# A decode layer on one core: shared weights kept on TensorE, w1 loaded early, the last value products placed by landing, the last cast on two engines

## The chip, the cores and the metric

The kernel runs on one core of a Trainium2 chip. The metric is the device time of one execution in microseconds (us); the kernel before takes 529.73 us (median of three runs, 529.25 to 531.3). The profile's own span, from the first to the last instruction, is some 2.1 us shorter than the time (527.6 us in the profiled run of before); I keep the two apart and call them "time" and "span".

## The reference

A parallel block in one decode step: attention over the last 2048 of 8192 cached positions, a SwiGLU feed-forward net, and the residual, for four sequences of one token each.

```python
B, D, H, Sk, Dh, F = 4, 640, 32, 8192, 192, 1536     # bf16 throughout
xn = layernorm(x)                                     # [4, 640]
W  = min(4096, max(256, Sk // 4))                     # 2048
q  = xn @ wq                                          # [4, 32*192]
k, v = k_cache[:, :, Sk-W:], v_cache[:, :, Sk-W:]     # [4, 32, 2048, 192] each
o  = softmax(q . k * Dh**-0.5) . v                    # per head
out = x + o @ wo + (silu(xn @ w1) * (xn @ w3)) @ w2   # [4, 640]
```

K and V are 4 x 32 x 2048 x 192 x 2 bytes = 100.7 MB each. With the weights the kernel reads 222.97 MB and does little arithmetic with them.

## The kernel before

K and V of one head are 3.1 MB each and come in one transfer per head, K into two buffers, V into three. For each head the scores are made in four quarters: VectorE multiplies K with the broadcast q, TensorE adds the six slices of 32 products by matmuls with the identity, VectorE reduces the remaining 32.

```python
def mult(u):                       # u = head*4 + quarter; VectorE, 1.75 us
    pr = ppool.tile([P, JQ, Dh], BF16, tag="pr")
    nc.vector.tensor_tensor(out=pr[:], in0=kts[h][:, g*JQ:(g+1)*JQ, :], in1=qbc[...], op=ALU.mult)

def adder(u):                      # TensorE: six matmuls, all with the same weights idb
    for kk in range(NK):
        nc.tensor.matmul(ps[:], lhsT=idb[:], rhs=pr[:, :, kk*DD:(kk+1)*DD],
                         start=(kk == 0), stop=(kk == NK-1))

def pv(h, j0=0, j1=NJ):            # 32 value products, weights = the head's probabilities z
    for jj in range(j0//2, j1//2):
        nc.tensor.matmul(o_ps[c*CT:c*CT+2*B, :], lhsT=z[:, 2*jj:2*jj+2, :], rhs=vt[:, 2*jj:2*jj+2, :], ...)
    ...
    nc.scalar.copy(out=o_sb[:], in_=o_ps[:])
```

All instructions are placed by hand in slots, one slot per quarter (128 of them and a tail). Within a slot a phase number orders them. Each engine gets its instructions in this order. The parts of the schedule that the change touches:

```python
ends = {H-3: (NU-1, NU+1), H-2: (NU+2, NU+3), H-1: (NU+6, NU+7)}   # slots of pv, ge_sum
for h in range(H):
    if h >= KBUFS: add((h-KBUFS+1)*GQ, 0, load_k, h)
    if h < H-2:    add(u0+2, 0, load_v, h)
    ...
    v, m = ends.get(h, (u0+L, u0+L+1))
    # h < H-1: add(v, 7, pv, h);  the last head in two halves, slots v-1 and v
    add(m, 7, ge_sum, h)
f = FFN_HEAD * GQ                          # FFN_HEAD = 6
add(f, 0, ffn_load, "w1", B_w1);     add(f+7, 7, ffn_in, "w1")
add(f+8, 0, ffn_load, "w3", B_w3);   add(f+15, 7, ffn_in, "w3")
... # at the end, in this order on the queue: V30, V31 (two halves), w2 part 0, wo 6, wo 7, w2 parts 1 and 2
res = ppool.tile([NR, N0], BF16, tag="pr", name="res")
nc.vector.tensor_copy(out=res[:], in_=acc[0:NR, :])
nc.sync.dma_start(out=out_v[:, 0:N0], in_=res[0:B, :])
nc.scalar.dma_start(out=out_v[:, N0:D], in_=res[CT:NR, :])
```

The last two heads are 30 and 31; "K31", "pv30" and so on name their loads and products. In the profile's names `kt` is K, `vt` is V, `pr` the products, `ps` the adder's sums, `o_ps` the value products, `acc` the final sum; both feed-forward input weights and w2 appear as `w`.

Of the kernel before, what the change touches and what calls it, by code (L numbers as in the profile page):

```python
# [12 lines left out]
ALU = mybir.AluOpType  # L13
ACTF = mybir.ActivationFunctionType
AX = mybir.AxisListType


@with_exitstack
def kernel(
# [15 lines left out]
    VBUFS: int = 3,  # L35
    PBUFS: int = 4,
    L: int = 8,
    FFN_HEAD: int = 6,
):
    nc = tc.nc  # L40
    P = 128
    B, Sq, D = A_x.shape
    _, H, Sk, Dh = A_k_cache.shape
# [4 lines left out]
    PB = P // B  # L48
    NJ = W // PB
    GQ = 4  # L50
# [8 lines left out]
    NU = H * GQ  # L59
    N0 = D // 2  # L60
# [4 lines left out]
    assert (H * Dh) % QC == 0 and NQ % 6 == 0 and QW % P == 0 and Dh == CT * RPP and P == HG * CT and F == HG * CT * FC  # L65
    assert 2 * H * Dh <= NJ * Dh and KBUFS == 2 and VBUFS == 3

    ctx.enter_context(tc.manual_schedule())
    head = ctx.enter_context(tc.tile_pool(name="head", bufs=1))
    fpool = ctx.enter_context(tc.tile_pool(name="ffn", bufs=1))  # L70
# [15 lines left out]
    v_win = A_v_cache[:, :, Sk - W:Sk, :]  # L86
    kts, vts, prs, pss, scs, exs, zs = {}, {}, {}, {}, {}, {}, {}
# [5 lines left out]
                          in_=k_win[:, h].rearrange("b (p j) d -> p b (j d)", p=PB))  # L93
        kts[h] = kt

    def load_v(h, parts=1):
        vt = vpool.tile([P, NJ, Dh], BF16, tag="vt")
        src = v_win[:, h].rearrange("b (p j) d -> p b j d", p=PB)
        n = NJ // parts
        for j in range(0, NJ, n):  # L100
            nc.sync.dma_start(out=vt[:, j:j + n, :].rearrange("q j d -> q (j d)"),
                              in_=src[:, :, j:j + n, :].rearrange("p b j d -> p b (j d)"))
        vts[h] = vt

    def wo_load(hg):
# [8 lines left out]
    for k0 in range(0, KC, 2):  # L114
        n = min(2, KC - k0)
        wt = vpool.tile([P, 2, H * Dh], BF16, tag="vt")
        nc.sync.dma_start(out=wt[:, 0:n, :].rearrange("p k n -> p (k n)"),
                          in_=wq_v[:, k0:k0 + n, :].rearrange("p k n -> p (k n)"))
        wq_rows += [wt[:, i, :] for i in range(n)]
    for h in range(KBUFS):  # L120
# [9 lines left out]
    mask_f = const.tile([P, B], FP32, name="mask_f")  # L130
    nc.vector.tensor_reduce(out=mask_f[:], in_=idf[:].rearrange("q (p b) -> q b p", b=B), axis=AX.X, op=ALU.add)
    mask_b = const.tile([P, B], BF16, name="mask_b")
# [3 lines left out]
    nc.vector.tensor_reduce(out=rows[:], in_=idf[:].rearrange("q (c k) -> q k c", k=CT)[:, 0:2 * B, :],  # L136
                            axis=AX.X, op=ALU.add)
    NREP = CT // B
# [8 lines left out]
    ssum = const.tile([B, 1], FP32, name="ssum")  # L147
    nc.vector.tensor_reduce(out=ssum[:], in_=xf[:], axis=AX.X, op=ALU.add)
    negmean = const.tile([B, 1], FP32, name="negmean")
# [40 lines left out]
    o_banks = []  # L190
    for i in range(2):
        o_ps = ps_o.tile([P, 2 * Dh], FP32, tag="o_ps", name="o_ps")
# [3 lines left out]
    acc = ps_acc.tile([P, N0], FP32, name="acc")  # L196
# [37 lines left out]
    def reduce_quarter(u):  # L234
        h, g = u // GQ, u % GQ
        if g == 0:
            scs[h] = small.tile([P, NJ], FP32, tag="sc", name="sc")
        nc.vector.tensor_reduce(out=scs[h][:, g * JQ:(g + 1) * JQ], in_=pss.pop(u)[:], axis=AX.X, op=ALU.add)  # L238

    def chain_lmax(h):  # L240
        lmax = small.tile([P, 1], FP32, tag="lmax")
        nc.vector.tensor_reduce(out=lmax[:], in_=scs[h][:], axis=AX.X, op=ALU.max)  # L242
        chs[h] = [lmax]
# [6 lines left out]
    def chain_gmax(h):  # L250
        gmax = small.tile([1, B], FP32, tag="gmax")
        nc.vector.tensor_reduce(out=gmax[:], in_=chs[h][1][0:1, 0:P].rearrange("o (p b) -> o b p", b=B),  # L252
                                axis=AX.X, op=ALU.max)
        gneg = small.tile([1, PB, B], FP32, tag="gneg")
# [20 lines left out]
                                in1=mask_b[:].unsqueeze(1).to_broadcast([P, NJ, B]), op=ALU.mult)  # L275
        zs[h] = z

    def pv(h, j0=0, j1=NJ):
        o_ps, z, vt = o_banks[h % 2], zs[h], vts[h]
        for jj in range(j0 // 2, j1 // 2):  # L280
            c = jj % 4
            nc.tensor.matmul(o_ps[c * CT:c * CT + 2 * B, :], lhsT=z[:, 2 * jj:2 * jj + 2, :],  # L282
                             rhs=vt[:, 2 * jj:2 * jj + 2, :], start=(jj < 4), stop=(jj >= NJ // 2 - 4))
        if j1 < NJ:
            return
        zs.pop(h)
        vts.pop(h)
        o_sb = small.tile([P, 2 * Dh], FP32, tag="o_sb", bufs=2, name="o_sb")
        nc.scalar.copy(out=o_sb[:], in_=o_ps[:])  # L289
        o_sbs[h] = o_sb  # L290
# [76 lines left out]
    def add(slot, phase, fn, *args):  # L367
        sched[slot].append((phase, len(sched[slot]), fn, args))



    ends = {H - 3: (NU - 1, NU + 1), H - 2: (NU + 2, NU + 3), H - 1: (NU + 6, NU + 7)}
    for h in range(H):
        u0, ul = h * GQ, h * GQ + GQ - 1
        if h >= KBUFS:
            add((h - KBUFS + 1) * GQ, 0, load_k, h)
        if h < H - 2:
            add(u0 + 2, 0, load_v, h)
        for u in range(u0, ul + 1):
            add(u, 1, mult, u)  # L380
            add(u + 1, 2, adder, u)
            add(u + 1, 8, reduce_quarter, u)
        add(ul + 1, 9, chain_lmax, h)
        add(ul + 2, 3, chain_tr, h)
        add(ul + 2, 4, chain_gmax, h)
        add(ul + 3, 3, chain_bc, h)
        add(ul + 3, 4, chain_z, h)
        add(ul + 4, 5, ge_tot, h)
        if h % HG == HG - 1:
            add(ul + 4, 9, ge_rec, h // HG)  # L390
        v, m = ends.get(h, (u0 + L, u0 + L + 1))
        if h < H - 1:
            add(v, 7, pv, h)
        else:
            add(v - 1, 7, pv, h, 0, NJ // 2)
            add(v, 7, pv, h, NJ // 2, NJ)
        add(m, 7, ge_sum, h)
        if h % HG == HG - 1:
            add(m + 1, 0, ge_turn, h // HG)
    e = ends[H - 1][1] + 1  # L400
    for hg in range(NG - 2):
# [1 line left out]
        add(hg * HG * GQ + 8, 0, wo_load, hg)  # L403
        add(a, 6, ge_proj, hg, 0, RPP // 2)
        add(a + 1, 6, ge_proj, hg, RPP // 2, RPP)
    f = FFN_HEAD * GQ
    add(f, 0, ffn_load, "w1", B_w1)
    add(f + 7, 7, ffn_in, "w1")
    add(f + 7, 9, ffn_silu)
    add(f + 8, 0, ffn_load, "w3", B_w3)  # L410
    add(f + 15, 7, ffn_in, "w3")
    add(f + 15, 9, ffn_h)
    add(8, 0, x_load)
    add(16, 6, x_add, 0)
    add(17, 6, x_add, 1)


    for h in range(H - 2, H):
        add(NU - 6, 0, load_v, h, 1 + (h == H - 1))
    add(NU - 6, 0, w2_load, 0)  # L420
    add(NU - 6, 0, wo_load, NG - 2)
    add(NU - 6, 0, wo_load, NG - 1)
# [11 lines left out]

    NR = CT + B
    res = ppool.tile([NR, N0], BF16, tag="pr", name="res")
    nc.vector.tensor_copy(out=res[:], in_=acc[0:NR, :])
    out_v = out.rearrange("b s d -> (b s) d")
    nc.sync.dma_start(out=out_v[:, 0:N0], in_=res[0:B, :])
    nc.scalar.dma_start(out=out_v[:, N0:D], in_=res[CT:NR, :])  # L440
# [30 lines left out]
```

## Time and profile before

| | before |
|---|---|
| time, median of 3 | 529.73 us |
| span | 527.6 us |
| TensorE / VectorE busy | 67% / 65% |
| data queue, share of 16 DMA engines | 98.6% |
| bytes read | 222.97 MB |

The profile page of before, cut: busy time and instructions of TensorE (PE), bandwidth in 40 equal slices of the span, the DMA queues (packets, MB, share of 16 engines), and the adder's weight loads (busy us, mean ns | idle before, and what ended it).

```profile
span 527.6 us, 5428 instructions
PE 353.5 (67%) x2306; PEld 142.6 (27%) x2307; DVE 345.6 (65%) x435; ACT 45.6 (9%) x143; POOL 1.1 (0%) x8
...
GB/s 358 434 430 415 420 439 434 430 434 419 439 438 427 432 427 437 429 434 428 432 432 432 432 427 435 432 432 430 432 430 432 432 430 434 429 435 427 438 419 203
...
q1 hardware_dynamic: 11680, 222.97, 98.6%
q8 instruction: 18, 0.29, 0.2%
...
L230 PEld LDWEIGHTS <-idb 128*128 128x128 bf16 x768 | 74.4, 102 | 258.7 <-issue 200.1
```

The stream of data is the kernel: all slices but the first and the last show 415 to 439 GB/s, and 222.97 MB at 431 GB/s take about 517 of 527.6 us. The instruction queue q8, with its 18 packets (16 KiB and 0.88 to 0.97 us each in the trace), looks like nothing.

Windows of before around 40 us (columns: window, its length, busy us of each engine, granted clock, DMA share, GB/s):

```profile
40.00:44.00 4.00, 2.24 (x10) 0.87 (x9) 3.97 (x5) 0.00 (x0) 0.00 (x0) 1.00 0.91 369
44.00:48.00 4.00, 2.72 (x13) 1.25 (x12) 3.97 (x6) 0.27 (x2) 0.00 (x0) 1.00 1.06 455
```

From 40 to 44 us the rate falls to 369 GB/s: there is a hole. The same view at the end:

```profile
518.00:519.00 1.00, 1.00 (x20) 0.40 (x16) 0.17 (x1) 0.00 (x0) 0.00 (x0) 1.00 0.99 405
519.00:520.00 1.00, 0.99 (x17) 0.35 (x8) 0.00 (x0) 0.00 (x0) 0.00 (x0) 1.00 0.68 284
...
521.00:522.00 1.00, 1.00 (x24) 0.71 (x18) 0.00 (x0) 0.00 (x0) 0.00 (x0) 1.00 0.49 195
522.00:523.00 1.00, 0.65 (x11) 0.20 (x6) 0.80 (x2) 0.00 (x0) 0.00 (x0) 1.00 0.13 45
523.00:524.00 1.00, 0.95 (x15) 0.62 (x16) 0.00 (x0) 0.00 (x0) 0.00 (x0) 1.00 0.03 13
```

Here the 16 engines do not stop together. The share goes from 0.99 to about 0.5 near 519 us (seven of them are done), stays there for over two microseconds, and a last engine works alone until 523.5 us. What TensorE and VectorE do meanwhile, from the timeline of before (start us, us, engine, line, operation, operands, count, and in brackets the idle time before and what ended it):

```profile
490.16 1.47 PE L230 MATMUL ps<-pr,idb 128*128 128x512 bf16 x6
...
498.64 1.76 DVE L219 TENSOR_TENSOR pr<-kt,qbc 128x3072 bf16<-128x3072 bf16 x1 [2.71 <-DMA kt<-in_A_k_cache_dram]
...
513.82 2.73 PE L282 MATMUL o_ps<-vt,z 128*8 128x384 bf16 x32
...
524.62 0.48 DVE L437 CAST res<-acc 36x320 bf16<-36x320 f32 x1 [1.62 <-PE acc L200]
525.13 0.30 SPq L439 DMA_DIRECT2D out_dram<-res  x1
```

The first line is one adder: six matmuls in 1.47 us. K31 lands at 498.64 us. The 32 products of pv30 take 2.73 us from 513.82 on (the granted clock is 0.50 from 514 to 516 us), pv31, the sums and the projection come behind them, and the last cast starts at 524.62, over 1.1 us after the last byte. The chain of waits of before (start, us, what) says the same: it ends in computation, not in a transfer.

```profile
522.62 0.39 DVE oT L315
...
523.05 1.54 PE acc L200 x20
...
524.62 0.48 DVE res L437
```

### The profile page before, as it was taken

Reading aid. Unit: us, or ns where it says so; the run is one execution under the profiler, and the core shown is the slowest. Engines: PE = TensorE matmul, PEld = TensorE weight load, DVE = VectorE, ACT = ScalarE, POOL = GpSimd, SP = SyncE. Lnnn points to the kernel's source line nnn. Section 1 sums busy time; section 2 is a strip of 40 time slices with the busy share of each in tenths; the row PEclk is TensorE's granted clock in tenths of the full one; section 3 lists DMA queues with packets and bytes.
Section 4 is the critical chain, followed back from the end, with each engine's and each line's share of the span. In section 5 each row is a group of like instructions: output and inputs, shape, how many; then the busy total and the mean of one; then the engine's idle time right before and its main releaser. Section 6 shows DMA issues by size and latency. Waiting matters only on the chain.

```text
span 527.6 us, 5428 instructions
## 1 busy us (share of the span) xinstructions
PE 353.5 (67%) x2306; PEld 142.6 (27%) x2307; DVE 345.6 (65%) x435; ACT 45.6 (9%) x143; POOL 1.1 (0%) x8
## 2 busy tenths in 40 slices
PE   2865886765657476577637866577566777675686
PEld 0322332322212232223212322223222332232233
DVE  3179775776458567686637876577657867677661
ACT  2111000100211000000000000000000000000010
POOL 0000000000000000000000000000000000000000
PEclk9889887899878989789997998789997988799788
DMA  8999999999999999999999999999999999999994
GB/s 358 434 430 415 420 439 434 430 434 419 439 438 427 432 427 437 429 434 428 432 432 432 432 427 435 432 432 430 432 430 432 432 430 434 429 435 427 438 419 203
DMA packets 11719, 223.31 MB, mean 423 GB/s; under 512 B 1312, under 2 KB 1328, under 8 KB 2608
## 3 DMA queue, kind: packets, MB, share of 16 engines
q1 hardware_dynamic: 11680, 222.97, 98.6%
q8 instruction: 18, 0.29, 0.2%
q14 instruction: 5, 0.04, 0.0%
q10 hardware_dynamic: 16, 0.01, 0.0%
HBM read 222.96 MB, written 0.01 MB: 423 GB/s over the span
## 4 chain that ended last, share of the span: by engine, by line
DMA 57%; DVE 22%; PE 18%; ACT 2%; issue 1%; SPq 0%
DMA kt<-in_A_k_cache_dram 54%; DVE pr L219 15%; PE ps L230 9%; PE po L307 4%; DVE sc L238 3%; DMA wt<-in_A_wq_dram 3%; PE qps L179 2%; PE o_ps L282 2%; DVE z L274 1%; ACT ex L266 1%; PE mt L260 1%; DVE oT L315 1%; DVE og L312 0%; PE acc L200 0%; ACT L266 0%
## 5 line engine op out<-in xcount | busy, mean ns | idle before, releaser
L230 PE MATMUL ps<-pr,idb 128*128 128x512 bf16 x768 | 208.5, 412 | 152.3 <-DVE pr L219 152.3
L219 DVE TENSOR_TENSOR pr<-kt,qbc 128x3072 bf16<-128x3072 bf16 x128 | 223.5, 1746 | 113.9 <-DMA kt<-in_A_k_cache_dram 113.9
L230 PEld LDWEIGHTS <-idb 128*128 128x128 bf16 x768 | 74.4, 102 | 258.7 <-issue 200.1
L238 DVE TENSOR_REDUCE sc<-ps 128x16 f32<-128x512 f32 x128 | 87.2, 681 | 2.0 <-PE ps L230 2.0
L282 PE MATMUL o_ps<-vt,z 128*8 128x384 bf16 x1024 | 60.6, 373 | 2.7 <-DMA vt<-in_A_v_cache_dram 2.7
L307 PE MATMUL po<-o_sb,sel_w 128*32 128x192 f32 x128 | 49.1, 517 | 1.1 <-ACT o_sb L289 1.1
L282 PEld LDWEIGHTS <-z 128*8 128x8 bf16 x1024 | 26.2, 94 | 32.8 <-issue 22.8
L289 ACT COPY o_sb<-o_ps 128x384 f32<-128x384 f32 x32 | 15.3, 479 | 189.7 <-PE o_ps L282 189.7
L274 DVE TENSOR_TENSOR z<-ex,mask_b 128x256 bf16<-128x256 bf16 x32 | 13.5, 422 | 22.0 <-ACT ex L266 22.0
L263 ACT COPY negm<-mt 128x1 f32<-128x1 f32 x32 | 5.1, 159 | 259.0 <-PE mt L260 259.0
L307 PEld LDWEIGHTS po<-o_sb,sel_w 128*32 128x32 f32 x128 | 13.6, 128 | 26.8 <-issue 25.0
L179 PE MATMUL qps<-wt,xnT 128*128 128x512 bf16 x59 | 17.2, 456 | 4.8 <-DMA wt<-in_A_wq_dram 4.7
L185 DVE CAST qbc<-qps 128x512 bf16<-128x512 f32 x6 | 3.8, 684 | 18.7 <-PE qps L179 18.7
L260 PEld LDWEIGHTS mt<-ones_ff,gneg 1*128 1x128 f32 x64 | 9.5, 186 | 13.8 <-issue 11.7
L252 DVE TENSOR_REDUCE gmax<-mt 1x4 f32<-1x128 f32 x32 | 8.8, 275 | 6.6 <-PE mt L247 6.6
L260 PE MATMUL mt<-ones_ff,gneg 1*128 1x1 f32 x64 | 12.2, 258 | 0.0
L247 PE MATMUL mt<-idf,lmax 128*1 128x128 f32 x32 | 10.6, 330 | 1.1 <-DVE lmax L242 1.1
L266 ACT ACTIVATE ex<-sc,negm 128x64 bf16<-128x64 f32 x32 | 11.1, 348 | 1.0
L179 PEld LDWEIGHTS <-xnT 128*128 128x128 bf16 x60 | 6.7, 112 | 14.8 <-issue 9.7
L200 PE MATMUL acc<-wo_t,oT 128*4 128x320 bf16 x96 | 9.2, 298 | 0.4 <-DVE oT L315 0.4
L294 PEld LDWEIGHTS po<-rsum,tot_w 128*32 128x32 f32 x64 | 4.6, 110 | 14.1 <-issue 12.5
L242 DVE TENSOR_REDUCE lmax<-sc 128x1 f32<-128x64 f32 x32 | 7.0, 220 | 1.1
(52 smaller groups left out, 64.2 us busy)
## 6 DMA issues: line engine op xcount, KB each, us to landing
kt<-in_A_k_cache_dram SPq DMA_DIRECT2D x32, 3072.0 KB, 19.0
vt<-in_A_v_cache_dram SPq DMA_DIRECT2D x31, 3072.0 KB, 26.1
wo_t<-in_A_wo_dram SPq DMA_DIRECT2D x8, 960.0 KB, 20.5
wt<-in_A_wq_dram SPq DMA_DIRECT2D x2, 3072.0 KB, 13.3
w<-in_B_w_dram SPq DMA_DIRECT2D x2, 1920.0 KB, 27.1
vt<-in_A_v_cache_dram SPq DMA_DIRECT2D x2, 1536.0 KB, 31.2
wt<-in_A_wq_dram SPq DMA_DIRECT2D x1, 1536.0 KB
w<-in_B_w_dram SPq DMA_DIRECT2D x1, 1280.0 KB, 33.6
```

What stands on the lines that cost most here:

```text
L179: nc.tensor.matmul(qp[:], lhsT=xnT[:, kc].rearrange("p a b -> p (a b)"), rhs=wq_rows[kc][:, (c0 + i) * QC:(c0 + i + 1) * QC], start=(kc == ...
L200: nc.tensor.matmul(acc[i * CT:i * CT + B, :], lhsT=lhsT, rhs=rhs[:, i * N0:(i + 1) * N0], start=first, stop=last)
L219: nc.vector.tensor_tensor(out=pr[:], in0=kts[h][:, g * JQ:(g + 1) * JQ, :], in1=qbc[:, h * Dh:(h + 1) * Dh].unsqueeze(1).to_broadcast([P, ...
L230: nc.tensor.matmul(ps[:], lhsT=idb[:], rhs=pr[:, :, kk * DD:(kk + 1) * DD], start=(kk == 0), stop=(kk == NK - 1))
L238: nc.vector.tensor_reduce(out=scs[h][:, g * JQ:(g + 1) * JQ], in_=pss.pop(u)[:], axis=AX.X, op=ALU.add)
L247: nc.tensor.transpose(out=mt[0:1, 0:P], in_=chs[h][0][:], identity=idf[:])
L260: nc.tensor.matmul(mt[:, P:P + 1], lhsT=gneg[:].rearrange("o p b -> o (p b)"), rhs=ones_ff[0:1, 0:1], start=True, stop=True)
L266: nc.scalar.activation(out=ex[:], in_=scs.pop(h)[:], func=ACTF.Exp, bias=negm[:, 0:1], scale=SCALE, accum_out=rsum[:])
L274: nc.vector.tensor_tensor(out=z[:], in0=ex[:].unsqueeze(2).to_broadcast([P, NJ, B]), in1=mask_b[:].unsqueeze(1).to_broadcast([P, NJ, B]), ...
L282: nc.tensor.matmul(o_ps[c * CT:c * CT + 2 * B, :], lhsT=z[:, 2 * jj:2 * jj + 2, :], rhs=vt[:, 2 * jj:2 * jj + 2, :], start=(jj < 4), stop= ...
L289: nc.scalar.copy(out=o_sb[:], in_=o_ps[:])
L307: nc.tensor.matmul(po[sl, 0:Dh], lhsT=sel_w[:, par].rearrange("p a b -> p (a b)"), rhs=o_sb[:, par * Dh:(par + 1) * Dh].rearrange("p (r i) ...
```

## The change

Its intent: TensorE need not load the identity again for each of six matmuls; w1 fills a gap between V0 and K2 in the queue; pv29, pv30 and pv31 are placed when their data land, so that only pv31 is left behind the last scores; two engines share the last cast.

```diff
+def keep_loaded_weights(nc):
+    for f in nc.python_module().functions:
+        for block in f.blocks:
+            held, again = None, []
+            for i, ins in enumerate(block.instructions):
+                if isinstance(ins, mybir.InstLdweights):
+                    key = (str(ins.ins[0]), ins.tile_position, ins.tile_size, ins.perf_mode, ins.is_transpose)
+                    if key == held and not ins.has_wait() and not ins.has_update():
+                        again.append(i)
+                    held = key
+                elif isinstance(ins, mybir.InstMatmult) and ins.ldweights is not False:
+                    held = None
+            for i in reversed(again):
+                del block.instructions[i]
...
+    nc.at_finalize(keep_loaded_weights)
...                                        (load_v and pv lose their halves: one V31 transfer, one pv31)
-    ends = {H - 3: (NU - 1, NU + 1), H - 2: (NU + 2, NU + 3), H - 1: (NU + 6, NU + 7)}
+    ends = {H - 2: (NU - 1, NU), H - 1: (NU + 3, NU + 4)}
...
-    f = FFN_HEAD * GQ
-    add(f, 0, ffn_load, "w1", B_w1)          # and ffn_in at f+7; w3 at f+8, f+15
+    add(3, 0, ffn_load, "w1", B_w1)
+    add(11, 7, ffn_in, "w1")
+    add(15, 0, ffn_load, "w3", B_w3)
+    add(23, 7, ffn_in, "w3")
...
-    nc.vector.tensor_copy(out=res[:], in_=acc[0:NR, :])
+    nc.vector.tensor_copy(out=res[:, 0:N0 // 2], in_=acc[0:NR, 0:N0 // 2])
+    nc.scalar.copy(out=res[:, N0 // 2:N0], in_=acc[0:NR, N0 // 2:N0])
```

More of the change, by code (lines that the diff above doesn't have):

```diff
@@ L37 @@
     L: int = 8,
-    FFN_HEAD: int = 6,
 ):
@@ L94, in load_k, with load_v @@
         kts[h] = kt
-    def load_v(h, parts=1):
+    def load_v(h):
         vt = vpool.tile([P, NJ, Dh], BF16, tag="vt")
-        src = v_win[:, h].rearrange("b (p j) d -> p b j d", p=PB)
-        n = NJ // parts
-        for j in range(0, NJ, n):
-            nc.sync.dma_start(out=vt[:, j:j + n, :].rearrange("q j d -> q (j d)"),
-                              in_=src[:, :, j:j + n, :].rearrange("p b j d -> p b (j d)"))
+        nc.sync.dma_start(out=vt[:].rearrange("q j d -> q (j d)"),
+                          in_=v_win[:, h].rearrange("b (p j) d -> p b (j d)", p=PB))
         vts[h] = vt
@@ L276, in chain_z, with pv @@
         zs[h] = z
-    def pv(h, j0=0, j1=NJ):
-        o_ps, z, vt = o_banks[h % 2], zs[h], vts[h]
-        for jj in range(j0 // 2, j1 // 2):
+    def pv(h):
+        o_ps, z, vt = o_banks[h % 2], zs.pop(h), vts.pop(h)
+        for jj in range(NJ // 2):
             c = jj % 4
@@ L283, in pv @@
                              rhs=vt[:, 2 * jj:2 * jj + 2, :], start=(jj < 4), stop=(jj >= NJ // 2 - 4))
-        if j1 < NJ:
-            return
-        zs.pop(h)
-        vts.pop(h)
         o_sb = small.tile([P, 2 * Dh], FP32, tag="o_sb", bufs=2, name="o_sb")
@@ L391 @@
         v, m = ends.get(h, (u0 + L, u0 + L + 1))
-        if h < H - 1:
-            add(v, 7, pv, h)
-        else:
-            add(v - 1, 7, pv, h, 0, NJ // 2)
-            add(v, 7, pv, h, NJ // 2, NJ)
+        add(v, 7, pv, h)
         add(m, 7, ge_sum, h)
@@ L405 @@
         add(a + 1, 6, ge_proj, hg, RPP // 2, RPP)
-    f = FFN_HEAD * GQ
-    add(f, 0, ffn_load, "w1", B_w1)
-    add(f + 7, 7, ffn_in, "w1")
-    add(f + 7, 9, ffn_silu)
-    add(f + 8, 0, ffn_load, "w3", B_w3)
-    add(f + 15, 7, ffn_in, "w3")
-    add(f + 15, 9, ffn_h)
+    add(3, 0, ffn_load, "w1", B_w1)
+    add(11, 7, ffn_in, "w1")
+    add(11, 9, ffn_silu)
+    add(15, 0, ffn_load, "w3", B_w3)
+    add(23, 7, ffn_in, "w3")
+    add(23, 9, ffn_h)
     add(8, 0, x_load)
@@ L418 @@
     for h in range(H - 2, H):
-        add(NU - 6, 0, load_v, h, 1 + (h == H - 1))
+        add(NU - 6, 0, load_v, h)
     add(NU - 6, 0, w2_load, 0)
```

## The prediction

> **What bounds the kernel.** The DMA engines. The queue table gives the data queue 98.6% of 16 engines' span and 222.97 MB; windows of 20 us from 60 to 500 us all show 428 to 433 GB/s, and 222.97 MB at 431 GB/s is 517 us of the 527.6 us span. PE is 67% busy, DVE 65%. Time can only come from a hole, stragglers, and what follows the last byte.
>
> **What the change does.**
> 1. Weight loads. Compiled, PE falls from 4168 to 2780 rows (identity loads 770 to 126, xnT 100 to 50). Six adder matmuls take 1.46 us warm, 243 ns each[...].[...] Almost none is critical: PE waits for DVE, DVE for K, K for the queue.
>    A side effect counts for more.[...] 18 instruction packets of 16 KiB, 0.88 to 0.97 us each, and the data packet behind each is stretched by some 0.5 us: about 1.4 us lost on one engine per block. The engines finish in groups: about half near 519.2 us, half near 522.0, one at 523.5; spacings of 2.8 and 1.4 us look like zero, two and three blocks. 1388 fewer rows should leave 12 or 13 packets, so the last straggler should come about 1.4 us earlier.
> 2. The hole. V0 lands at 42.5 to 43.1 us but K2 is issued only at 41.10 and starts late; windows show 369 GB/s from 40 to 44 us. w1 (1.97 MB, 4.6 us of stream), issued behind V0, fills it: about 0.45 us on most engines, perhaps less on the straggler.
> 3. The tail. Now the chain from K31's landing (498.64) is compute: adder, softmax chain, pv(30) at half clock (2.7 us), pv(31), sums, turn, projection, cast at 524.62; the last byte landed at 523.5. After, pv(30) runs before the last adder, so only pv(31) follows z31 (now at 515.0). Estimate from the durations: turn done near 520.5, before the last w2 piece lands. The tail then waits for DMA: last landing, four matmuls, cast.
> 4. The cast: 0.48 us becomes two halves side by side, about 0.33 us.
>
> **Sum.** Landing 523.5 -> about 522.0 (straggler 1.4, hole 0.1 to 0.45); the cast starts 0.6 us after it instead of 1.1; cast 0.15 shorter; output DMA unchanged. Together -2.1 us, 0.4%. The FFN work only moves.
>
> **Prediction: 527.6 us (from 529.73), 8 in 10 between 526.0 and 529.6 us.** Faster by over 2%: 0.01; within 2%: 0.98; slower: 0.01.
>
> **What would show it.** Adders near 1.3 us when warm, PE busy lower by 15 to 30 us at nearly the same span; 12 or 13 packets in the instruction queue; no dip near 40 to 44 us; the chain of waits ending DMA w2 -> PE acc -> cast, 0.6 us from last landing to cast; casts of about 0.3 us.
>
> **What would make it wrong.** Block fetches falling on the straggler as often as before (gain about 1 us); the tail's PE still at half clock so that compute ends it;[...] run-to-run spread (529.25 to 531.3) as large as the effect. A gain over 2% would need less traffic or a faster stream, which nothing here touches.

Some passages are cut from it: a time for a matmul without its load and the saving on TensorE worked out from that, a rule for the size of instruction fetches, and a remark about the clock. No trace or run here shows them. None was a term of the sum, which is complete: the last landing 1.5 us earlier (straggler 1.4, hole 0.1 to 0.45), the cast 0.5 us closer behind it, 0.15 us off the cast, together -2.1 us, from 529.73 to 527.6. The "blocks" are the instruction packets; 12 or 13 of them agrees with an estimate from before: 4168 rows of its compiled listing with 18 packets are 232 rows a packet, and 2780 rows then need about 12. That PE waits for DVE and DVE for K is in the waits of before: 152.3 us before the adders and 113.9 us before the products.

## The result, and the profile after

The changed kernel takes 527.53 us (median of four runs, 527.38 to 527.64) against 529.6 us for before (four runs): 2.1 us less. The ratio is 0.9952, 95% interval 0.9933 to 0.9972. Ratios are computed from the mean time of one kernel's fast runs over that of the other's in the same rounds, so they are not quite the ratio of the medians I quote. The interval lies below 1. The outputs are right.

The profile page after, the same lines:

```profile
span 525.5 us, 4734 instructions
PE 354.6 (67%) x2307; PEld 74.0 (14%) x1613; DVE 345.2 (66%) x435; ACT 45.9 (9%) x144; POOL 1.1 (0%) x8
...
GB/s 360 430 438 425 440 431 424 436 428 439 425 433 431 435 426 432 434 427 439 430 427 440 425 434 430 436 428 435 432 428 434 430 430 436 430 434 430 434 422 240
...
q1 hardware_dynamic: 11536, 222.97, 98.9%
q8 instruction: 15, 0.25, 0.2%
...
L244 PEld LDWEIGHTS <-idb 128*128 128x128 bf16 x124 | 11.9, 96 | 39.1 <-issue 32.6
```

TensorE's busy time has not fallen at all (353.5 before, 354.6 after), though its weight loads of the identity went from 768 to 124 records. The instruction queue went from 18 packets to 15. The hole:

```profile
40.00:44.00 4.00, 2.38 (x11) 0.00 (x0) 3.96 (x6) 0.00 (x0) 0.00 (x0) 1.00 0.96 410
44.00:48.00 4.00, 2.58 (x13) 0.57 (x5) 3.97 (x6) 0.41 (x2) 0.00 (x0) 1.00 0.99 425
```

410 GB/s instead of 369 from 40 to 44 us. The end of the stream:

```profile
518.00:519.00 1.00, 1.00 (x21) 0.65 (x17) 0.15 (x1) 0.00 (x0) 0.00 (x0) 1.00 0.79 325
519.00:520.00 1.00, 0.67 (x10) 0.30 (x7) 0.65 (x2) 0.00 (x0) 0.00 (x0) 1.00 0.53 215
...
521.00:522.00 1.00, 0.73 (x14) 0.35 (x8) 0.00 (x0) 0.00 (x0) 0.00 (x0) 1.00 0.13 51
522.00:523.00 1.00, 0.27 (x4) 0.00 (x0) 0.32 (x1) 0.28 (x1) 0.00 (x0) 1.00 0.00 0
```

The same shape, about two microseconds earlier: nothing is left after 522 us. The timeline after:

```profile
505.43 1.47 PE L244 MATMUL ps<-pr,idb 128*128 128x512 bf16 x6
...
506.91 1.46 PE L296 MATMUL o_ps<-vt,z 128*8 128x384 bf16 x29
...
522.31 0.32 DVE L442 CAST res<-acc 36x160 bf16<-36x160 f32 x1 [2.63 <-PE acc L214]
522.66 0.28 ACT L443 CAST res<-acc 36x160 bf16<-36x160 f32 x1 [5.48 <-DVE res L442]
522.97 0.30 SPq L445 DMA_DIRECT2D out_dram<-res  x1
```

The adder at 505.43 takes 1.47 us, exactly as before. pv30 (506.91) now runs before the last adder. The cast in two halves runs one half behind the other: ScalarE starts at 522.66, after VectorE has ended, and the output is sent at 522.97. The chain of waits after:

```profile
490.75 31.04 DMA w<-in_B_w_dram
...
521.83 0.45 PE acc L214 x4
...
522.31 0.33 DVE res L442
...
522.66 0.28 ACT res L443
```

It now ends in the transfer of w2, then four matmuls, then the two halves in a row.

One more reading, worked out from the trace's records of DMA packets. A large transfer ends with 16 packets of 4 bytes (9 ns each in before and after), which I read as one completion on each of the 16 engines; these are the times (us) of those of the last piece of w2, and the three experiments below belong beside them (the bars are mine, between groups):

```
before             518.9 519.2 519.2 519.2 519.3 519.3 519.7 | 521.5 521.6 521.7 522.0 522.0 522.1 522.1 522.2 | 523.5
after              518.3 518.3 518.4 518.5 518.7 519.0 519.2 519.7 | 521.1 521.2 521.3 521.3 521.3 521.3 521.4 521.5
x5_loads_moved     518.2 518.3 518.4 518.6 518.7 518.8 518.9 | 521.0 521.2 521.2 521.2 521.3 521.4 521.4 | 522.9 522.9
x9_loads_tail      518.9 518.9 519.0 519.2 519.2 519.4 519.7 520.4 | 521.5 521.8 521.8 521.8 521.8 521.9 522.0 522.6
x10_more_blocks    518.2 518.4 518.5 518.7 518.8 518.8 519.2 | 521.4 | 522.5 522.6 522.7 522.7 522.8 | 524.2 524.2 524.4
```

### The profile page after: what moved, and what is told of

Same layout as the page of the kernel before. It is cut to its first block, busy times and chain, and to the rows that moved or that the text cites. A ratio compares the mean times of both kernels' runs of the same rounds, so it can differ in the third digit from the quotient of the medians.

```text
span 525.5 us, 4734 instructions
## 1 busy us (share of the span) xinstructions
PE 354.6 (67%) x2307; PEld 74.0 (14%) x1613; DVE 345.2 (66%) x435; ACT 45.9 (9%) x144; POOL 1.1 (0%) x8
## 3 DMA queue, kind: packets, MB, share of 16 engines
q1 hardware_dynamic: 11536, 222.97, 98.9%
## 4 chain that ended last, share of the span: by engine, by line
DMA 66%; PE 17%; DVE 14%; ACT 2%; issue 1%; SPq 0%
DMA kt<-in_A_k_cache_dram 52%; PE ps L244 10%; DVE pr L233 10%; DMA w<-in_B_w_dram 6%; DMA vt<-in_A_v_cache_dram 5%; PE po L317 4%; DMA wt<-in_A_wq_dram 4%; DVE sc L252 2%; PE qps L193 1%; ACT ex L280 1%; DVE z L288 1%; PE mt L274 1%; PE mt L261 0%; ACT negm L277 0%; DVE qbc L199 0%
## 5 line engine op out<-in xcount | busy, mean ns | idle before, releaser
L244 PE MATMUL ps<-pr,idb 128*128 128x512 bf16 x768 | 211.5, 417 | 151.0 <-DVE pr L233 151.0
L296 PE MATMUL o_ps<-vt,z 128*8 128x384 bf16 x1024 | 57.4, 365 | 0.2 <-DVE z L288 0.2
L261 PEld LDWEIGHTS mt<-idf,lmax 128*1 128x1 f32 x32 | 3.2, 100 | 140.8 <-issue 140.8
L193 PE MATMUL qps<-wt,xnT 128*128 128x512 bf16 x60 | 16.1, 428 | 5.1 <-DMA wt<-in_A_wq_dram 5.1
L244 PEld LDWEIGHTS <-idb 128*128 128x128 bf16 x124 | 11.9, 96 | 39.1 <-issue 32.6
L304 PE MATMUL po<-rsum,tot_w 128*32 128x1 f32 x64 | 7.1, 181 | 1.3 <-ACT ex L280 1.3
```

The costliest lines, as they stand in the source:

```text
L193: nc.tensor.matmul(qp[:], lhsT=xnT[:, kc].rearrange("p a b -> p (a b)"), rhs=wq_rows[kc][:, (c0 + i) * QC:(c0 + i + 1) * QC], start=(kc == ...
L244: nc.tensor.matmul(ps[:], lhsT=idb[:], rhs=pr[:, :, kk * DD:(kk + 1) * DD], start=(kk == 0), stop=(kk == NK - 1))
L261: nc.tensor.transpose(out=mt[0:1, 0:P], in_=chs[h][0][:], identity=idf[:])
L296: nc.tensor.matmul(o_ps[c * CT:c * CT + 2 * B, :], lhsT=z[:, 2 * jj:2 * jj + 2, :], rhs=vt[:, 2 * jj:2 * jj + 2, :], start=(jj < 4), stop= ...
L304: nc.tensor.matmul(po[sl, Dh:Dh + 1], lhsT=tot_w[:].rearrange("p a b -> p (a b)"), rhs=rsums.pop(h)[:], start=True, stop=True)
```

## The experiments

The theory (A in the expectations): the time is the start, a stream of fixed speed (428 to 433 GB/s in every 20 us from 60 to 500 us of before), plus what the slowest of 16 DMA engines loses, plus what follows its last byte. By this theory the removed loads count because they are instructions that come through the same DMA engines as the data, not because they cost TensorE time. The trace of before shows the two in each other's way: beside 14 of the 18 instruction packets a data packet of 24 KiB takes 1.38 to 1.46 us, where the median is 0.91. The rivals: the loads cost TensorE time (B); the loads do nothing (C); the tail's order is the whole gain (D). All runs have five rounds. Some comparisons are between runs on different chips, and say so: the medians of before on the three chips were 529.54, 530.11 and 529.46 us, so differences of half a microsecond between chips are weak by the times alone. (The changed kernel gave 527.53 us in the result and 527.57 in a0.)

### x1_loads_only: before, with the repeated loads taken out

```diff
+    nc.at_finalize(keep_loaded_weights)
```

> The kernel before with only the repeated weight loads taken out (694 fewer instructions on TensorE). Theory A (instruction blocks set the slowest DMA engine): 15 instruction packets of 16 KiB instead of 18, the last data packet ends about 1.4 us earlier (523.5 to about 522.1), the landing of K31 too, and the span falls by 1.2 to 1.6 us (527.6 to about 526.2). Rival B (the loads cost TensorE time in the final chain): packets are incidental; K31 lands when it did, and the gain is what the last adders and sums save, 0.2 to 0.5 us. Rival C (only the tail order and the hole matter): no gain, under 0.2 us.

Measured: 529.69 us, median of six, against 529.54: no gain, ratio 1.0005 (0.9985 to 1.0026), but a wide scatter, from 528.38 to 531.77. The profiled run (span 526.8) had the 15 packets and the last data at 522.1 us, as A says, yet the cast started only at 523.84, in the chain of waits:

```profile
523.84 0.48 DVE res L455
```

It stood behind the old tail's computation, 1.7 us after the last data. So the expected fall of 1.2 to 1.6 us is a miss as a median. By itself this run would have spoken for C.

### x2_w1_only: before, with w1 and w3 early

```diff
-    add(f, 0, ffn_load, "w1", B_w1)      # f = 24
+    add(3, 0, ffn_load, "w1", B_w1)      # ffn_in at 11, w3 at 15, its ffn_in at 23
```

> The kernel before with only w1 and w3 loaded early. The hole at 42.6 us closes (no stretch below 400 GB/s from 40 to 44 us, w1 lands 4.6 us behind V0 and K2 another 7.3 us behind it). Theory A: all engines were within 0.5 us of each other there, so all of them gain the 0.5 us, and the span falls by 0.4 to 0.6 us; 18 packets stay. Rival: the slowest engine is late for another reason and never idled, gain under 0.15 us.

Measured: 528.93 us (528.55 to 529.4) against 529.54; ratio 0.9987 (0.9971 to 1.0002), span 527.0. In the packet records V0 completes at 42.5 to 43.2 us, w1 at 47.0 to 47.8, K2 from 54.3 on: 4.56 and 7.3 us apart, so the stream has no hole. In before, K2 completed 7.6 us and more behind V0. The size is that of A, 0.6 us, though the interval just includes no change. Also, no run exceeded 529.4, where the eleven of before went up to 531.43.

### x3_tail_only: before, with the new tail

```diff
-    ends = {H - 3: (NU - 1, NU + 1), H - 2: (NU + 2, NU + 3), H - 1: (NU + 6, NU + 7)}
+    ends = {H - 2: (NU - 1, NU), H - 1: (NU + 3, NU + 4)}      # and V31 in one transfer
```

> The kernel before with only the last value products moved (pv30 ahead of the last adder, V31 in one transfer). Theory A: the last data packet stays at 523.5 us and becomes what ends the chain; the cast starts 0.8 us behind it instead of 1.1, gain 0.2 to 0.4 us. Rival D (the compute chain of the tail was what the whole change bought): gain of 1 us or more.

Measured: 529.75 us (529.48 to 530.39) against 529.54, ratio 1.0003 (0.9989 to 1.0017). The last data came at 523.57 and the cast started at 524.43 instead of 524.62: 0.2 us, lost in the scatter of the times. In the chain of waits:

```profile
524.43 0.48 DVE res L442
```

The expected gain of 0.2 to 0.4 us does not show in the median. D is out: the order of the tail alone buys nothing, because the slowest DMA engine ends at the same time (523.57 us here, 523.5 in before).

### x6_after_with_loads: the changed kernel with all loads back

```diff
-    nc.at_finalize(keep_loaded_weights)
```

> The changed kernel with all weight loads back (694 more instructions). Theory A: 18 packets again, last data packet 1.3 to 1.5 us later than in the changed kernel (521.5 to about 523.0), span 526.8 to 527.0 against 525.5, that is only 0.6 to 0.9 us better than before. Rival C: as good as the changed kernel within 0.2 us.

Measured: 529.15 us (528.69 to 529.35), 1.6 us above the changed kernel's 527.57 (on another chip); profiled span 526.9, last data at 522.84. So with the hole filled and the new tail, the loads do count, by about the expected amount. Against before in the same rounds it gains only 0.4 us, where 0.6 to 0.9 was expected; its interval (0.9975 to 1.0002) just includes no gain. The instruction queue of this kernel, from its page:

```profile
q8 instruction: 18, 0.29, 0.2%
```

C is out. What x6 cannot say is whether the loads or their fetch cost the time.

### x5_loads_moved: as many loads, but not between the matmuls

Instead of deleting a repeated load, this kernel moves it behind the last matmul of its group, where TensorE mostly waits for VectorE (147 us of its idle time before the adders of x5 end with VectorE's products). (Plain no-operation instructions in their place: the compiler dropped them.)

```diff
-            for i in reversed(again):
-                del block.instructions[i]
+            # each repeated load goes in front of the next load (or self-loading matmul) that is kept
+            for at, late in reversed(moves):
+                for i in reversed(late):
+                    ins = block.instructions[i]
+                    block.instructions.insert(at, ins)
+                    del block.instructions[i]
+                    at -= 1
```

> The changed kernel with its 694 repeated weight loads put back, but behind the last matmul of each group instead of between the matmuls, where TensorE mostly waits for VectorE: as many instructions as with the loads in place (4209 against 4239), yet matmuls run without a load between them. Theory A (instruction blocks): 17 or 18 packets, span about 526.9, as slow as the changed kernel with its loads in place, 1.2 to 1.6 us worse than the changed kernel. Rival B (loads between matmuls cost the time): as fast as the changed kernel within 0.3 us, whatever the packets.

Its page has the 18 packets again, and its timeline an adder without any load inside:

```profile
q8 instruction: 18, 0.29, 0.2%
```

```profile
491.13 1.47 PE L252 MATMUL ps<-pr,idb 128*128 128x512 bf16 x6
```

The adder takes 1.47 us as in both other kernels. Measured: 528.92 us (528.72 to 529.44) against 527.57 (527.35 to 527.65) for the changed kernel in the same rounds: 1.35 us slower, with no overlap of the runs. B is out as far as "between the matmuls" goes: the loads cost as much in the new place, so their presence counts. In the profiled run two engines end late, at 522.9 us: the 18th instruction packet starts at 521.6 us, on an engine that still had a data packet to move.

### x10_more_blocks: more instructions still

```diff
     def adder(u):
         ...
+        if u < NU - 8:
+            for _ in range(20):
+                nc.tensor.ldweights(idb[0:B, 0:B])     # four columns, never used
```

> The changed kernel with the loads moved behind the groups, and 20 more idle loads of four columns behind each group (2400 more instructions, 6609 on TensorE), none in the last eight groups. Theory A: 27 or 28 packets of instructions, so some engine takes one more of them than with 18, the last data packet 1.3 to 1.5 us later than with the loads moved, time 530.2 to 530.6 us against 528.92. Rival (what slows is loads at those places on TensorE, or nothing): within 0.3 us of the loads moved, as TensorE has idle time behind each group.

The loads moved as in x5, and 2400 idle ones added. Its page and its last windows:

```profile
q8 instruction: 27, 0.44, 0.3%
```

```profile
522.00:523.00 1.00, 0.59 (x11) 0.17 (x4) 0.80 (x2) 0.00 (x0) 0.00 (x0) 1.00 0.38 154
523.00:524.00 1.00, 0.87 (x14) 0.68 (x16) 0.00 (x0) 0.00 (x0) 0.00 (x0) 1.00 0.19 77
524.00:525.00 1.00, 0.67 (x10) 0.21 (x7) 0.00 (x0) 0.00 (x0) 0.00 (x0) 1.00 0.04 15
```

There are 27 packets (3545 instructions on TensorE came with 15, 4239 with 18 and these 6609 with 27, that is 236, 235 and 245 a packet), and the share, 0.13 between 522 and 523 us in before and zero in the changed kernel, is still 0.38 here. Measured: 530.29 us (530.22 to 530.45), 1.37 us above x5 (on another chip; in the profiles the last data came 1.47 us later): the expected 530.2 to 530.6. 694 more instructions cost 1.35 us in x5 and 2400 more cost 1.37 here, so the cost does not follow the number of instructions. By the times alone it could still follow the busy time of the loads, which the profile pages give as 74.0 us in the changed kernel, 108.6 in x5 and 138.9 here. The completion times speak against that: seven engines end at 518.2 to 519.2 us, as in the changed kernel, so the stream as a whole was not held up, and only some of its engines were.

The completion times in the block above show the steps: in every kernel seven or eight engines end near 518.5 us (0.5 us later where the hole is); the others at about 521.3, 522.7 and 524.2, that is 2.8, 4.2 and 5.7 us later. With about 1.4 us for one packet of instructions (an estimate from before: 0.88 to 0.97 us for the packet, and the 0.5 us by which a data packet beside it is longer) that is two, three and four of them.

Three more readings of the packet records support this. First, the delay of one engine by one packet can be seen directly: here the first instruction packet starts at 40.2 us, and of the 16 completions of V0 fifteen come at 42.3 to 43.1 us and one at 44.4. Second, the durations of the instruction packets repeat with a period of eight in all thirteen profiles (in before 967, 949, 884, 879, 935, 933, 928, 961 ns, then 961, 955, 880, 886, 936, 940, 921, 960, then 961, 947; in after 936, 921, 964, 960, 947, 881, 886, 934, then 929, 921, 962, 961, 947, 879, 879), as if eight engines took them in turn. Third, the counts then fit, by an estimate from that period: 15 packets give seven engines two and one engine one (perhaps the engine at 519.7 us in after and 520.4 in x9); 18 give two engines a third, and two end late in x2, x3, x5 and x6 (in before the 18th starts at 522.2 us, on an engine that has just finished, and only one ends late); 27 give three engines a fourth and five a third, just the 5 and 3 in the last row. That eight engines take them, and the same eight each time, is inferred and not shown, as the trace does not name the engine of a packet. One more engine ends with those of two packets (521.4 us in the last row) and stays unexplained; the five packets of q14 may be why.

### x8_loads_w1: the changed kernel with the old tail (and one cast)

Before, with the edits of x1 and x2 together.

> The kernel before with two parts of the change: repeated loads taken out and w1 early; old order of the tail, one cast. Against the changed kernel with one cast (527.36 us, span 525.3 to 525.6) it lacks only the tail order. Theory A: 15 packets, last data packet at 521.4 to 521.8 us, but the compute chain of the old tail ends 0.3 to 0.6 us later than DMA allows, so span 525.7 to 526.2 and the time steady within 0.5 us from run to run (loads alone ran from 528.38 to 531.77: with the hole). Rival: loads without the tail order gain nothing, as loads alone did in the median, span 526.8 or more.

Measured: 528.13 us (527.54 to 529.02), against 527.36 for the changed kernel with one cast (x4, another chip): 0.8 us. I expected it to be steady; it is not, its spans run from 525.4 to 526.9. In the profiled run the last data came at 521.59, and the chain ended in the old tail:

```profile
522.10 1.54 PE acc L218 x20
...
523.66 0.48 DVE res L454
```

The cast starts two microseconds after the last byte. So the tail's order, worth nothing alone (x3), is worth about 0.8 us in the median once the stream ends earlier, and up to 1.7 us in single runs. The rival fails too: loads and w1 without the new tail gain 1.3 us over before in the same rounds.

### x9_loads_tail: the changed kernel with the hole (and one cast)

The changed kernel with one cast, w1 and w3 at their old slots.

> The kernel before with loads taken out and the new tail, one cast, but w1 late, so that the hole at 42.6 us stays: the changed kernel with one cast lacks only the w1 move against it. Theory A: the hole costs 0.5 us in the good runs and makes others worse: median span 526.0 to 526.8, with single runs 1 to 3 us above the best as in before and in loads alone (steps of about 1 us). Rival (the scatter belongs to the old tail): steady within 0.5 us.

The window of the hole in this kernel:

```profile
40.00:44.00 4.00, 2.22 (x10) 0.00 (x0) 3.96 (x5) 0.00 (x0) 0.00 (x0) 1.00 0.89 338
```

The rate falls to 338 GB/s there, as the hole asks. Measured: 527.99 us, five runs from 527.87 to 528.62 and one at 530.06, against 527.36 (x4, another chip): the hole costs about 0.6 us, and one of six runs shows the outlier that A expected. Its median span, 526.0, is at the lower edge of what was expected.

### a0_after, x4_one_cast, x7_two_tiles: the cast

The changed kernel again, and two versions of its end:

```diff
 x4
-    nc.vector.tensor_copy(out=res[:, 0:N0 // 2], in_=acc[0:NR, 0:N0 // 2])
-    nc.scalar.copy(out=res[:, N0 // 2:N0], in_=acc[0:NR, N0 // 2:N0])
+    nc.vector.tensor_copy(out=res[:], in_=acc[0:NR, :])
 x7
+    res_a = ppool.tile([B, N0], BF16, tag="pr", name="res_a")
+    res_b = ppool.tile([NR, N0], BF16, tag="pr", name="res_b")
+    nc.vector.tensor_copy(out=res_a[:], in_=acc[0:B, :])
+    nc.scalar.copy(out=res_b[CT:NR, :], in_=acc[CT:NR, :])
     # SyncE sends res_a, ScalarE sends its own res_b
```

> The changed kernel once more, as the yardstick for the other three on this chip: span 525.4 to 525.7 us, 2.0 us better than before.

> The changed kernel with the last cast on VectorE alone again. In the changed kernel's trace ScalarE's half waits for VectorE's half (0.33 and 0.28 us one behind the other, 0.66 us from the last matmul to the output transfer), the single cast took 0.48 us. Theory A: 0.15 us faster than the changed kernel. Rival: the two halves overlap in runs without the profiler and the single cast is 0.15 us slower.

> The changed kernel with the two casts split by output half into two tiles of their own (VectorE 4 rows of 320, ScalarE the other 4), so that no cast waits for the other and each engine sends its own half. Theory A (the wait came from the shared tile): the casts start together, 0.48 us from last matmul to the output transfer instead of 0.66, 0.15 to 0.25 us better than the changed kernel, equal to the single cast or a little better. Rival (the wait comes from both reading one accumulator): no better than the changed kernel.

Measured in the same rounds: the changed kernel 527.57 us (527.35 to 527.65), one cast 527.36 (527.11 to 527.73), two tiles 527.30 (527.17 to 527.39). The timelines of x4 and of x7:

```profile
522.60 0.48 DVE L442 CAST res<-acc 36x320 bf16<-36x320 f32 x1 [2.47 <-PE acc L214]
523.11 0.30 SPq L444 DMA_DIRECT2D out_dram<-res  x1
```

```profile
522.29 0.48 DVE L443 CAST res_a<-acc 4x320 bf16<-4x320 f32 x1 [3.26 <-PE acc L214]
522.32 0.42 ACT L444 CAST res_b<-acc 4x320 bf16<-4x320 f32 x1 [5.77 <-PE acc L214]
...
522.79 0.30 SPq L446 DMA_DIRECT2D out_dram<-res_a  x1
```

In x4 the output leaves 0.51 us after the cast starts; in the changed kernel it was 0.66 (522.31 to 522.97). In x7 both casts start within 0.03 us of each other, both reading the accumulator, so reading it together is not what made one wait; the wait most likely came from writing one tile. (x7 also splits by rows where the changed kernel splits by columns, and no run separates the two.) The gains, 0.2 and 0.3 us, are about those expected; they are at the edge of what these times resolve. x7 is the fastest kernel: 2.8 us below the 530.11 of before in its rounds, ratio 0.9949 (0.9934 to 0.9964).

## Why the prediction was right or wrong

The time was right: 527.6 us predicted, 527.53 measured. The steps, one by one:

1. **DMA bounds the kernel, and only the edges of the stream can move.** Right. The data queue's share went from 98.6% to 98.9%, and the slices between the first and the last show 422 to 440 GB/s after 415 to 439.
2. **Weight loads cost TensorE time: adders near 1.3 us without them, 15 to 30 us less busy.** Wrong. I divided 1.46 us by six, got 243 ns, and set against it a time for a matmul without its load that no trace here shows. But the last matmul of a group counts with its full duration, 379 ns in the trace (whose matmul ends are modelled); the starts inside a group are 215 ns apart before and after, with a load in front of every matmul and without (median of the trace's adder matmuls at the full granted clock, called warm). 5 x 215 + 379 = 1454 ns: the loads were already hidden, also at the full clock. TensorE's busy time therefore stayed at 354 us, and an adder at 1.47 us. The time did not suffer, because the prediction counted none of this in its sum.
3. **Fewer instruction packets, so the slowest engine ends 1.4 us earlier.** Right, and the largest part: with the loads back but moved out of the way x5 loses 1.35 us, x6 gives 1.6 us, and x10 a step of 1.37 us in the other direction; that it is their fetch rests on the packet records under x10. The count was off: I said 1388 fewer rows and 12 or 13 packets; the listing I counted in merges equal neighbours, the program lost 694, and 15 packets came. It made no difference to the time, which was luck: if eight engines take the packets in turn (an estimate from the period of eight in their durations), no engine gets a third one until the 17th.
4. **The hole is worth 0.1 to 0.45 us.** Its mechanism is right, its size a little small: 0.6 us in x2 (where the interval just includes no change) and in x9 (across chips), about 0.5 us in the completion times of the engines. I doubted that the slowest engine had idled; at 43 us all 16 were still within 0.6 us of each other, so all of them had.
5. **After the change the chain ends with the transfer of w2.** Right, but I had 0.6 us from the last landing to the cast; from the last data at 521.52 to the cast at 522.31 it was 0.8. The new order's worth depends on the rest: nothing alone, 0.8 us with the other parts.
6. **The cast becomes 0.15 us shorter.** Wrong. The two halves write one tile, and the second waits for the first. From its start to the output transfer it takes 0.66 us instead of 0.51: about 0.15 us more in the trace, 0.2 by the medians.

The sum came out because the misses were small and cancelled, which is luck: in the profiled runs the last landing moved by 2.0 us (predicted 1.5), the wait from there to the cast shrank by 0.3 (predicted 0.5), and the cast took 0.15 more (predicted 0.15 less). The parts do not add up, either alone (0, 0.6, 0) or taken out of the whole (1.6, 0.6, 0.8, and -0.2 for the cast): the tail ends with the later of a transfer and a computation, and a gain on one side shows only when the other has been moved too.

What stays open: why before, x1 and x9 (all with the hole) and x8 (with the old tail) scatter by 1.5 to 3.4 us from run to run while the changed kernel stays within 0.3. The hole alone does not decide it: x3 has it too and stays within 0.9 us. For x8 the later end of the computation is shown in one profile, but not what makes it differ between runs; for the hole no profile of a slow run was taken.

## What to carry to other kernels

When a kernel is bound by its transfers, count its instructions too: here they came through the same DMA engines (18 packets instead of 15 cost 1.35 us in x5), and the slowest engine set the end. Before crediting a removed instruction with its busy time, look at the distance between the starts of its neighbours, in the middle of a group (here 215 ns with the load and without). A part of a change that shows nothing alone can be worth its full amount once the path beside it is shortened, so test it also by taking it out of the whole. And two engines that wrote one tile took turns here (0.66 us from the first cast's start to the output, 0.50 with a tile each in x7), so try giving each its own.
